# Gates spread by transposes of a broadcast column, the third group's y tiles rounded in one go, and one more drain of GpSimd

## The chip, the core and the metric

The kernel runs on one core of one Trainium2 chip. The metric is the device time of one execution in microseconds (us). Engines: PE is TensorE, ACT is ScalarE, DVE is VectorE, POOL is GpSimd, SP is SyncE, which here issues the plain DMAs. PEld is TensorE's weight load.

## The reference

Three layers follow each other: chunked attention with memory tokens, a top-1 mixture of experts, and an MLP with a SiLU. The change lies in the third, and in how the second's result reaches it. With N = 3072 tokens, D = 512, and a hidden width of 2048:

```python
def _moe_ref(x, expert_emb, tau, w1, w2):
    ...                                   # logits, argmax, softmax
    gate_w = probs[np.arange(N), expert_idx]
    for e in range(E):
        mask = expert_idx == e
        h = np.maximum(x[mask] @ w1[e], 0.0)
        out[mask] = gate_w[mask, None] * (h @ w2[e])

def _moe2_ref(x, w_in, w_out):
    h = x @ w_in
    g = h * (1.0 / (1.0 + np.exp(-h)))
    return (g @ w_out).astype(np.float32)
```

The gate of a token, gate_w, is one number. Here it is multiplied in ahead of the third layer, onto y = h @ w2[e].

## The kernel before, in words

Precision comes from splitting: a float32 tile is written as a high part rounded to fp32r and a low part, the rest, and each product is three matmuls, high x high, high x low and low x high (`three`, L101 to L103; `split`, L96 and L97).

The mixture of experts leaves y in DRAM (`ys`), transposed, in the order of the experts' slots; `names_d` holds which token stands at each place, and `gd` the gate of each token. The third layer takes the tokens in NG = 6 groups of GT2 = 512 (TG = 4 blocks of 128). Group 0 is gated and turned before; its tiles lie in `yt[0]`. For a group g >= 1 these steps are made:

- `load_names(g)`: SP loads the 512 token names to `tok_i`; `load_y(g)`: SP loads 1 MB of y to `yraw`, as KD = 4 blocks of 128 x 512 (model dimension on partitions, tokens on columns).
- `pick_gates(g)`: GpSimd gathers the gates of the 4 x 128 tokens from `gd` to four columns of `gt` (tokens on partitions), one indirect DMA a column.
- To multiply y, the gates must lie along the columns, the same on all 128 partitions. For g = 1, `diagonal` and `spread_gates` do it: ScalarE scales the identity's rows by the gates, and a matmul with a tile of ones sums the columns into `bank[0]`. For g >= 2, `list_gates` has SP store `gt` to DRAM (`gates_d`) and `load_gates` loads it back to `ygate[g]`, repeated over the partitions.
- `gate_y(g, k)`: VectorE multiplies block k of `yraw` by `ygate[g]` (L1270). `high_y` (ScalarE, L1273) and `low_y` (VectorE, L1277) write the rounded tiles to `yt[g % 2]`.

Groups 0 to 2 run through a loop of NI2 = 48 steps i, one for each group and block f of 128 hidden units; the order is `steps`: group 0 for f = 0 to 7, group 1, group 0 for f = 8 to 15 (i = 24 to 31), group 2 from i = 32. A step is written out by hand: what `prep[i]` holds; `up(i + 1)` (12 matmuls of 512 columns to `bank[2]` or `bank[3]`, then the sigmoid on ScalarE, L1216); `silu(i + 1)` (VectorE, L1221) and `halves(i + 1)` (the split to gh and gl); `add(i, c)` for the four blocks of tokens (12 matmuls to `bank[4]` to `bank[7]`); and what `late[i]` holds. `bank[0]` and `bank[1]` are free in the loop. `yt[0]` holds group 0 until `up(31)` and group 2 from `up(32)` on, so at i = 30 the tiles of group 2 are rounded between the two. In steps 22 to 31 VectorE and ScalarE also build mixed weights (`mix`, `mix_halves`).

Groups 3 to 5 (GM = 3) run through `product(q)`, NP2 = 8 products a group, each for two blocks of hidden units. `up2` makes seven half-size products (`seven`: 6 matmuls of 256 columns each) to the left halves of `bank[0]` to `bank[3]` and the right halves of `bank[0]` to `bank[2]`; the right half of `bank[3]` is free. Their mixed weights come from `mixed_d` through a ring of five slots, three in `ring` and two in `y0` (shown as y): `load_mixed(q)` has SP load 256 KB for each of four slots two products ahead (L1386), each waiting for the matmuls that read the slot before. `after_q[q]` lists what product q does ahead of its `up2`: for the group that comes next (g = 4 and 5) the names and y at product 1, pick_gates and list_gates at 2, load_gates at 3, gate_y at 4 and 5. At a group's end `give` copies each block of 128 tokens out of its bank and GpSimd scatters it to `out` by an indirect DMA (L1244). L1595 is the call of the kernel: what shows there at the end are the drains and the barrier behind the program.

All engines take their instructions in the order of this code. SP issues a DMA only when what it waits for is done, and all that SP has to issue stands behind it.

Of the kernel before, what the change touches and what calls it, by code (L numbers as in the profile page):

```python
# [59 lines left out]
def tile_chunk_attention_top1_moe_silu_mlp(ctx, tc, qT, kT, vW, emb, tau, wm, wo, out):  # L60
# [11 lines left out]
    gates_d = dram.tile([N, 1], F32, name="gates_d")  # L72
# [1117 lines left out]
    with ExitStack() as a:  # L1190
# [12 lines left out]
        ygate = [None, bank[0]]  # L1203
# [79 lines left out]
        def list_gates(g):  # L1283
            t = (g - 1) * TG
            SP.dma_start(
                out=gates_d[t * P:(t + TG) * P].rearrange("(c p) o -> p (c o)", p=P), in_=gt[:, 0:TG]
            )

        def load_gates(g):
            at = (g - 1) * GT2  # L1290
            SP.dma_start(out=ygate[g], in_=gates_d[at:at + GT2].rearrange("n o -> o n").to_broadcast([P, GT2]))

        diag, ones = held[0].rearrange("p (c t) -> p c t", c=TG), held[1][:, 0:P]

        def diagonal():
            for c in range(TG):
                ACT.activation(diag[:, c], ident, AF.Copy, scale=gt[:, c:c + 1])

        def spread_gates():
            for c in range(TG):  # L1300
                PE.matmul(bank[0][:, c * P:(c + 1) * P], ones, diag[:, c], start=True, stop=True)

        POOL.memset(ones, 1.0)
# [6 lines left out]
        prep[4].append(diagonal)  # L1310
        late[4].append(spread_gates)
# [8 lines left out]
        for g in range(2, GM + 1):  # L1320
            at = 8 if g == 2 else (g - 1) * NF2 + 1
            prep[at].append(lambda g=g: load_names(g))
            prep[at].append(lambda g=g: load_y(g))
            for n, do in enumerate((pick_gates, list_gates, load_gates)):
                prep[at + (2, 4, 16 if g == 2 else 7)[n]].append(lambda g=g, do=do: do(g))
            if g == 2:
                plan_parts(g, [(gate_y, k) for k in range(KD)], 26, 1)
            elif g == GM:
                plan_parts(g, [(gate_y, k) for k in range(KD)], at + 8, 2)
# [8 lines left out]
        def sums():  # L1338
            less = lambda to, x, y: DVE.tensor_tensor(to, x, y, op=ALU.subtract)
            t1, t2, t4 = (block(t) for t in (held[3], ygate[GM], r_o[3]))  # L1340
            less(t1, quarter(1), quarter(0))
            less(quarter(1), quarter(3), quarter(1))
            yield
            less(t2, quarter(3), t1)
            less(t4, quarter(2), t2)
            yield

        def cast_block(n):
            src = (quarter(0), block(ygate[GM]), block(held[3]), quarter(1), quarter(2), quarter(3), block(r_o[3]))[n]
# [53 lines left out]
        after_q = defaultdict(list)  # L1403
        for g in range(GM + 1, NG):
            q = (g - GM - 1) * NP2
            for n, do in (1, load_names), (1, load_y), (2, pick_gates), (2, list_gates), (3, load_gates):
                after_q[q + n].append(lambda g=g, do=do: do(g))
            for k in range(KD):
# [55 lines left out]
        def product(q):  # L1464
# [9 lines left out]
            if p < NP2 - 1:  # L1474
# [8 lines left out]
                for n in range(2):  # L1483
                    add2(q, n)
                    halves2(q + 1, n)
                    if last:
                        for b in range(3) if n == 0 else range(3, 7):
                            cast_block(b)
                return
            if g < NG - 1:  # L1490
                add2(q, 0)
                add2(q, 1)
                for c in range(TG):
                    give(g, c)

# [13 lines left out]
        for i in range(NI2):  # L1509
# [6 lines left out]
            if i == 2 * NF2 - 2:  # L1516
                for k in range(2):
                    high_y(2, k)
                    low_y(2, k)
            if i == HF - 1:  # L1520
# [8 lines left out]
            elif i + 1 < NI2:  # L1529
                silu(i + 1)  # L1530
                halves(i + 1)
            if i == coding[-1] + 1:
# [3 lines left out]
                ygate += [op.tile([P, GT2], F32, name="ygate")] * (NG - 2)  # L1536
# [9 lines left out]
            if i == 2 * NF2 - 2:  # L1546
                for k in range(2, KD):
                    high_y(2, k)
                    low_y(2, k)
# [49 lines left out]
```

## Time and profile before

| | |
|---|---|
| median of 3 runs | 995.09 us (992.78 to 995.28) |
| the profiled execution | 994.45 us, of which its span 992.6 us |
| busy TensorE / weight loads | 949.7 us (96%) / 849.2 us |
| busy VectorE / ScalarE / GpSimd | 717.2 / 474.6 / 148.1 us |
| TensorE's granted clock, mean | 0.993 |
| third layer: loop of groups 0 to 2 | from 464 us to about 728 us of the span |
| third layer: products of groups 3 to 5 | from about 728 us to about 983 us |

How to read it: the span runs from the first to the last instruction. Busy times are sums over the span; a matmul's end is modelled, so TensorE's stops are seen best in the starts of its matmuls. A wait names the engine that waited, its line, and what released it. SPq, POOLq and the like are an engine's sequencer: it issues DMAs, waits and drains, and the engine isn't counted as busy.

### The profile page before, as it was taken

The numbers are of one execution on the slowest core, as the hardware profiler recorded it, in microseconds if no ns is written. First come the engines' busy times: TensorE is split into PE (matmuls) and PEld (weight loads), VectorE is DVE, ScalarE is ACT, GpSimd is POOL, SyncE is SP. The second block draws the span as 40 slices with busy tenths as digits, with TensorE's granted clock in tenths as the row PEclk, the third lists the DMA queues.
The fourth block names the chain that finished last, engine by engine and source line by source line (L and its number), as shares of the span: only waits on it lengthen the run. The fifth ranks groups of instructions, "written<-read, shape, count | busy, mean of one in ns | idle before, by whom it ended". The sixth has DMA issues, their size and how long they took to land. (4 is left out here: it accounts for less than half of the span.)

```text
span 992.6 us, 19281 instructions
## 1 busy us (share of the span) xinstructions
PE 949.7 (96%) x7182; PEld 849.2 (86%) x7182; DVE 717.2 (72%) x1477; ACT 474.6 (48%) x925; POOL 148.1 (15%) x215
## 2 busy tenths in 40 slices
PE   6998989999999999998999999999998999999996
PEld 4776778999999999998888888788888989889994
DVE  8887797667777888896979986775464666566561
ACT  8896655445456666665454433332332233233231
POOL 8464122011030000010100001030012002001001
PEclk9999999999999999999999999999999999999998
DMA  8997646557477777874423313245053426634321
GB/s 298 365 364 249 247 157 227 177 193 234 129 252 241 249 261 257 274 255 163 147 86 80 113 54 127 86 170 127 0 179 104 124 79 190 128 92 133 122 76 42
DMA packets 65666, 169.97 MB, mean 171 GB/s; under 512 B 12246, under 2 KB 17936, under 8 KB 64536
## 3 DMA queue, kind: packets, MB, share of 16 engines
q1 hardware_dynamic: 60312, 153.91, 47.2%
q0 software_dynamic: 5248, 14.70, 4.6%
q8 instruction: 60, 0.98, 0.4%
q14 instruction: 46, 0.38, 0.2%
HBM read 141.02 MB, written 27.58 MB: 170 GB/s over the span
## 5 line engine op out<-in xcount | busy, mean ns | idle before, releaser
L101 PE MATMUL bank<-hhl,v2h 128*128 128x256 f32 (+1 forms) x352 | 105.0, 298 | 0.0
L102 PE MATMUL bank<-hll,v2h 128*128 128x256 f32 (+1 forms) x352 | 103.2, 293 | 0.0
L103 PE MATMUL bank<-hhl,v2l 128*128 128x256 f32 (+1 forms) x352 | 103.0, 293 | 0.0
L103 PE MATMUL bank<-w2bh,gl 128*128 128x512 f32 x224 | 87.2, 389 | 0.0
L101 PE MATMUL bank<-w2bh,gh 128*128 128x512 f32 x224 | 87.2, 389 | 0.0
L102 PE MATMUL bank<-w2bl,gh 128*128 128x512 f32 x224 | 87.2, 389 | 0.0
L1429 DVE TENSOR_TENSOR held<-held,bank 128x256 f32<-128x256 f32 x168 | 64.7, 418 | 28.8 <-PE bank L103 27.6
L186 ACT ACTIVATE hhl<-bank 128x256 fp32r<-128x256 f32 (+1 forms) x88 | 36.3, 412 | 91.9 <-PE bank L103 89.1
L97 DVE TENSOR_TENSOR w1l<-raw,w1h 128x512 fp32r<-128x512 f32 x106 | 72.6, 685 | 7.8 <-ACT w1h L96 4.9
L1244 POOL DMA_INDIRECT out_dram<-o,tok_i x20 | 20.4, 1019 | 380.6 <-DVE o L1241 324.0
L1216 ACT ACTIVATE sg<-bank 128x512 f32<-128x512 f32 x48 | 28.7, 598 | 100.5 <-PE bank L103 100.5
L187 DVE SCALAR_TENSOR_TENSOR hll<-bank,hhl 128x256 fp32r<-128x256 f32 (+1 forms) x88 | 40.2, 457 | 49.2 <-ACT hhl L186 48.8
L1420 ACT ACTIVATE sp<-held 128x512 f32<-128x512 f32 x48 | 29.5, 630 | 90.6 <-DVE held L1429 89.4
L97 DVE TENSOR_TENSOR v2l<-raw,v2h 128x512 fp32r<-128x512 f32 x106 | 72.7, 686 | 0.0
L101 PE MATMUL bank<-y,w2bh 128*128 128x512 f32 (+1 forms) x210 | 72.0, 343 | 0.0
L97 DVE TENSOR_TENSOR gl<-sp,gh 128x512 fp32r<-128x512 f32 x44 | 30.4, 692 | 57.5 <-ACT gh L96 57.4
L102 PE MATMUL bank<-y,w2bh 128*128 128x512 f32 (+1 forms) x210 | 71.9, 343 | 0.0
L103 PE MATMUL bank<-y,w2bl 128*128 128x512 f32 (+1 forms) x210 | 71.9, 343 | 0.0
L101 PE MATMUL bank<-xhl,w1h 128*128 128x256 f32 (+1 forms) x224 | 68.0, 304 | 2.5 <-PEq L1181 1.5
L152 POOL DMA_INDIRECT xrowl<-xd,rows_i x28 | 30.9, 1103 | 253.9 <-PE bank L174 211.8
L103 PE MATMUL bank<-xhl,w1l 128*128 128x256 f32 (+1 forms) x224 | 67.8, 303 | 0.2 <-DVE w1l L97 0.2
L102 PE MATMUL bank<-xll,w1h 128*128 128x256 f32 (+1 forms) x224 | 67.6, 302 | 0.0
(363 smaller groups left out, 2890.8 us busy)
## 6 DMA issues: line engine op xcount, KB each, us to landing
raw<-in_wm_dram SPq DMA_DIRECT2D x108, 512.0 KB, 4.1
coded<-in_wo_dram SPq DMA_DIRECT2D x36, 512.0 KB, 5.0
ring<-mixed_d SPq DMA_DIRECT2D x58, 256.0 KB, 3.9
vbuf<-in_vW_dram SPq DMA_DIRECT2D x32, 390.0 KB, 5.5
y<-mixed_d SPq DMA_DIRECT2D x38, 256.0 KB, 3.7
mixed_d<-stage SPq DMA_DIRECT2D x8, 1024.0 KB, 3.9
k<-in_kT_dram SPq DMA_DIRECT2D x16, 400.0 KB, 6.6
q<-in_qT_dram SPq DMA_DIRECT2D x16, 384.0 KB, 5.7
```

The lines of the kernel that those rows point to most:

```text
L97: eng.tensor_tensor(lo, src, hi.bitcast(F32), op=ALU.subtract)
L101: PE.matmul(out, lhsT=lh, rhs=rh, start=start, stop=False)
L102: PE.matmul(out, lhsT=lh, rhs=rl, start=False, stop=False)
L103: PE.matmul(out, lhsT=ll, rhs=rh, start=False, stop=stop)
L152: POOL.indirect_dma_start(out=s.where["row"][:, c], out_offset=None, in_=xd[0:LEAD * P] if s in pre else xd, in_offset=IndirectOffsetOnAxi ...
L186: ACT.activation(hh, h, AF.Relu)
L187: DVE.scalar_tensor_tensor(hl, h, 0.0, hh.bitcast(F32), op0=ALU.max, op1=ALU.subtract)
L1216: ACT.activation(sg, h, AF.Sigmoid)
L1244: POOL.indirect_dma_start(out=out, out_offset=IndirectOffsetOnAxis(ap=(tok_i[:, (g - 1) * TG + c:] if g else pre_i[:, c:])[:, 0:1], axis=0 ...
L1420: ACT.activation(out, src, AF.Sigmoid)
L1429: add = lambda to, x, y: DVE.tensor_tensor(to, x, y, op=ALU.add)
```

## The change

Gates of every group g >= 1 are spread by four transposes: the column `gt[:, c]`, read 128 times as a 128 x 128 tile, is transposed on TensorE with the identity. For g = 1, 2 and 3 they go to `bank[0]`, `bank[1]` and `bank[0]` in `late[4]`, `late[24]` and `late[39]`, and gate_y reads the bank. For g = 4 and 5 `spread_half` makes two transposes into the free half of `bank[3]` and ScalarE copies them to `ygate[g]`; the first pair stands ahead of the `up2` of product 3, the second at that product's end. `diagonal`, the tile of ones, `list_gates`, `load_gates` and `gates_d` go. At i = 30 all four `high_y` stand right behind `up(31)`, then two `low_y`, `silu(31)`, two `low_y`, `halves(31)`; the second half of them stood behind `add(30)`. Behind the gives of g = 4 GpSimd gets a `drain`.

```diff
--- before.py
+++ after.py
@@ -69,7 +69,6 @@
     xd = dram.tile([N, DM], F32, name="xd")
     ys = dram.tile([P, KD, N], F32, name="ys")
     names_d = dram.tile([N, 1], I32, name="names_d")
-    gates_d = dram.tile([N, 1], F32, name="gates_d")
     mixed_d = dram.tile([NF2 // 2, P, 4, DM], F32, name="mixed_d")
     gd = dram.tile([N, 1], F32, name="gd")
     td = dram.tile([(NA + 3 * N3) * P, 1], I32, name="td")
@@ -1200,7 +1199,7 @@
         yraw = wp.tile([P, KD, GT2], F32, name="yraw")
         gs = {}
         held = [hp.tile([P, DM], F32, name=f"held{c}") for c in range(TG)]
-        ygate = [None, bank[0]]
+        ygate = [None, bank[0], bank[1], bank[0]]
         HF = NF2 // 2
         steps = [(0, f) for f in range(HF)] + [(1, f) for f in range(NF2)] + [(0, f) for f in range(HF, NF2)]
         steps += [(g, f) for g in range(2, NG) for f in range(NF2)]
@@ -1280,35 +1279,17 @@
             for c in range(TG):
                 pick_gate(c, tok_i[:, (g - 1) * TG:])
 
-        def list_gates(g):
-            t = (g - 1) * TG
-            SP.dma_start(
-                out=gates_d[t * P:(t + TG) * P].rearrange("(c p) o -> p (c o)", p=P), in_=gt[:, 0:TG]
-            )
-
-        def load_gates(g):
-            at = (g - 1) * GT2
-            SP.dma_start(out=ygate[g], in_=gates_d[at:at + GT2].rearrange("n o -> o n").to_broadcast([P, GT2]))
-
-        diag, ones = held[0].rearrange("p (c t) -> p c t", c=TG), held[1][:, 0:P]
-
-        def diagonal():
-            for c in range(TG):
-                ACT.activation(diag[:, c], ident, AF.Copy, scale=gt[:, c:c + 1])
-
-        def spread_gates():
-            for c in range(TG):
-                PE.matmul(bank[0][:, c * P:(c + 1) * P], ones, diag[:, c], start=True, stop=True)
-
-        POOL.memset(ones, 1.0)
+        def spread_gates(to, part=range(TG)):
+            for n, c in enumerate(part):
+                PE.transpose(to[:, n * P:(n + 1) * P], gt[:, c:c + 1].to_broadcast([P, P]), ident)
+
         load_y(1)
         up(0)
         silu(0)
         halves(0)
         prep, late = defaultdict(list), defaultdict(list)
         prep[1].append(lambda: pick_gates(1))
-        prep[4].append(diagonal)
-        late[4].append(spread_gates)
+        late[4].append(lambda: spread_gates(ygate[1]))
         parting = [(gate_y, 0), (high_y, 0), (gate_y, 1), (high_y, 1), (low_y, 0), (gate_y, 2), (high_y, 2), (low_y, 1)]
         parting += [(gate_y, 3), (high_y, 3), (low_y, 2), (low_y, 3)]
 
@@ -1321,8 +1302,8 @@
             at = 8 if g == 2 else (g - 1) * NF2 + 1
             prep[at].append(lambda g=g: load_names(g))
             prep[at].append(lambda g=g: load_y(g))
-            for n, do in enumerate((pick_gates, list_gates, load_gates)):
-                prep[at + (2, 4, 16 if g == 2 else 7)[n]].append(lambda g=g, do=do: do(g))
+            prep[at + 2].append(lambda g=g: pick_gates(g))
+            late[24 if g == 2 else at + 6].append(lambda g=g: spread_gates(ygate[g]))
             if g == 2:
                 plan_parts(g, [(gate_y, k) for k in range(KD)], 26, 1)
             elif g == GM:
@@ -1337,7 +1318,7 @@
 
         def sums():
             less = lambda to, x, y: DVE.tensor_tensor(to, x, y, op=ALU.subtract)
-            t1, t2, t4 = (block(t) for t in (held[3], ygate[GM], r_o[3]))
+            t1, t2, t4 = (block(t) for t in (held[3], wide, r_o[3]))
             less(t1, quarter(1), quarter(0))
             less(quarter(1), quarter(3), quarter(1))
             yield
@@ -1346,7 +1327,7 @@
             yield
 
         def cast_block(n):
-            src = (quarter(0), block(ygate[GM]), block(held[3]), quarter(1), quarter(2), quarter(3), block(r_o[3]))[n]
+            src = (quarter(0), block(wide), block(held[3]), quarter(1), quarter(2), quarter(3), block(r_o[3]))[n]
             to = (Y11, Y2, Y1, Y3, Y21, Y22, Y4)[n]
             ACT.copy(block(to[0]), src)
             DVE.tensor_tensor(block(to[1]), src, block(to[0]).bitcast(F32), op=ALU.subtract)
@@ -1400,11 +1381,19 @@
         for n in range(2):
             prep[NI2 - 6].append(lambda n=n: next(adding[GM]))
 
-        after_q = defaultdict(list)
+        after_q, late_q = defaultdict(list), defaultdict(list)
+
+        def spread_half(g, n):
+            to = bank[3][:, QT:]
+            spread_gates(to, range(2 * n, 2 * n + 2))
+            ACT.copy(ygate[g][:, n * QT:(n + 1) * QT], to)
+
         for g in range(GM + 1, NG):
             q = (g - GM - 1) * NP2
-            for n, do in (1, load_names), (1, load_y), (2, pick_gates), (2, list_gates), (3, load_gates):
+            for n, do in (1, load_names), (1, load_y), (2, pick_gates):
                 after_q[q + n].append(lambda g=g, do=do: do(g))
+            for n, at in enumerate((after_q, late_q)):
+                at[q + 3].append(lambda g=g, n=n: spread_half(g, n))
             for k in range(KD):
                 after_q[q + 4 + k // 3].append(lambda g=g, k=k: gate_y(g, k))
             for n in range(2):
@@ -1486,12 +1475,16 @@
                     if last:
                         for b in range(3) if n == 0 else range(3, 7):
                             cast_block(b)
+                for do in late_q[q]:
+                    do()
                 return
             if g < NG - 1:
                 add2(q, 0)
                 add2(q, 1)
                 for c in range(TG):
                     give(g, c)
+                if g == NG - 2:
+                    POOL.drain()
 
         def hold_halves(q):
             for sg, to in zip(gs[q], (Y11, Y2)):
@@ -1514,9 +1507,14 @@
             if i + 1 < NI2:
                 up(i + 1)
             if i == 2 * NF2 - 2:
+                for k in range(KD):
+                    high_y(2, k)
                 for k in range(2):
-                    high_y(2, k)
                     low_y(2, k)
+                silu(i + 1)
+                for k in range(2, KD):
+                    low_y(2, k)
+                halves(i + 1)
             if i == HF - 1:
                 for c in range(TG):
                     add(i, c)
@@ -1526,14 +1524,15 @@
                 second_signs(j)
                 silu(i + 1)
                 second_split(j, lambda: halves(i + 1))
-            elif i + 1 < NI2:
+            elif i + 1 < NI2 and i != 2 * NF2 - 2:
                 silu(i + 1)
                 halves(i + 1)
             if i == coding[-1] + 1:
                 dx.close()
                 op = a.enter_context(tc.tile_pool(name="op", bufs=1))
                 r_o = [op.tile([P, DM], F32, name=f"o{c}") for c in range(TG)]
-                ygate += [op.tile([P, GT2], F32, name="ygate")] * (NG - 2)
+                wide = op.tile([P, GT2], F32, name="wide")
+                ygate += [wide] * (NG - 1 - GM)
                 ring = op.tile([P, 3, DM], F32R, name="ring")
                 ring = [ring[:, n] for n in range(3)] + [y0[:, n * GT2 + HOME:(n + 1) * GT2 + HOME] for n in (6, 7)]
             if i != HF - 1:
@@ -1543,10 +1542,6 @@
                         give(g, c)
             for do in late[i]:
                 do()
-            if i == 2 * NF2 - 2:
-                for k in range(2, KD):
-                    high_y(2, k)
-                    low_y(2, k)
         for q in range((NG - GM) * NP2):
             product(q)
```

## Rows read from the trace of the kernel before

**Rows 1.** TensorE's waits, 464 to 983 us: waiter, releaser; total us, times, longest.

```profile
PE bank L101 <- DMA ring<-mixed_d: 3.4, 2, 2.6
PE bank L102 <- DVE y L1277: 0.3, 1, 0.3
PE bank L101 <- ACT y L1273: 0.3, 1, 0.3
```

**Rows 2.** Timeline of SP's DMA queue: start us, length us, engine, line, count.

```profile
753.20 0.37 SPq L1285 DMA_DIRECT2D gates_d<-gt  x1
753.66 1.94 SPq L1386 DMA_DIRECT2D ring<-mixed_d  x2
...
763.29 0.32 SPq L1291 DMA_DIRECT2D ygate<-gates_d  x1
```

**Rows 3.** Timeline of TensorE at its two stops; in brackets idle us before, releaser.

```profile
765.36 0.28 PE L103 MATMUL bank<-y,ring 128*128 128x256 f32 x1
768.27 0.36 PE L101 MATMUL bank<-y,ring 128*128 128x256 f32 x1 [2.63 <-DMA ring<-mixed_d]
...
853.81 0.39 PE L101 MATMUL bank<-y,ring 128*128 128x256 f32 x1 [0.80 <-DMA ring<-mixed_d]
```

**Rows 4.** DMA issues: transfer, queue, count, KB each, median us to landing.

```profile
ring<-mixed_d SPq DMA_DIRECT2D x58, 256.0 KB, 3.9
...
gates_d<-gt SPq DMA_DIRECT2D x4, 2.0 KB, 11.7
```

**Rows 5.** Timeline of TensorE in the first `up` of group 2.

```profile
637.58 0.39 PE L102 MATMUL bank<-y,w2ah 128*128 128x512 f32 x1
637.81 0.39 PE L103 MATMUL bank<-y,w2al 128*128 128x512 f32 x1
...
639.61 0.40 PE L103 MATMUL bank<-y,w2al 128*128 128x512 f32 x1
```

**Rows 6.** Timeline of ScalarE at the same place.

```profile
634.71 1.13 ACT L1273 CAST y<-yraw 128x512 fp32r<-128x512 f32 x2
637.28 0.62 ACT L96 CAST gh<-sg 128x512 fp32r<-128x512 f32 x1 [1.44 <-DVE sg L1221]
637.80 1.14 ACT L1273 CAST y<-yraw 128x512 fp32r<-128x512 f32 x2
```

**Rows 7.** Timeline of VectorE at the same place.

```profile
635.35 1.29 DVE L1277 TENSOR_TENSOR y<-yraw,y 128x512 fp32r<-128x512 f32 x2 [1.08 <-ACT y L1273]
```

**Rows 8.** Timeline of TensorE at four transposes, and at the spreading of group 1.

```profile
330.49 0.60 PE L1133 MATMUL bank<-ident,yfirst 128*128 128x128 f32 x4
330.85 0.37 PE L101 MATMUL bank<-xhl,w1h 128*128 128x256 f32 x1
331.06 0.28 PE L102 MATMUL bank<-xll,w1h 128*128 128x256 f32 x1
...
494.14 1.05 PE L1301 MATMUL bank<-held,held 128*128 128x128 f32 x8
494.95 0.48 PE L101 MATMUL bank<-y,w2bh 128*128 128x512 f32 x1
```

**Rows 9.** The gating of y (line 1270): ns min/median/max, first and last start.

```profile
L1270 DVE TENSOR_TENSOR yraw<-yraw,ygate x16: 680/683/687, 609.6 to 873.8; 128x512 f32<-128x512 f32 x16
...
L1270 DVE TENSOR_TENSOR yraw<-yraw,bank x4: 679/679/680, 496.3 to 502.0; 128x512 f32<-128x512 f32 x4
```

**Rows 10.** Timeline of GpSimd, last group: first and last scatter.

```profile
971.95 0.97 POOL L1244 DMA_INDIRECT out_dram<-o,tok_i  x1 [57.83 <-DVE o L1241]
...
984.18 0.97 POOL L1244 DMA_INDIRECT out_dram<-o,tok_i  x1 [3.03 <-ACT o L1241]
```

**Rows 11.** The end (line 1595): count, ns min/median/max, first and last start.

```profile
L1595 POOLq DRAIN x3: 45/113/7818, 983.9 to 992.3; - x3
L1595 SPq DRAIN x3: 7/7/13, 987.5 to 992.0; - x3
```

**Rows 12.** GpSimd's sequencer behind the gathers of the experts (line 1181), same columns.

```profile
L1181 POOLq INC_SWDGE_SEM x2: 492/688/885, 235.5 to 440.6; - x2
```

## The prediction

> **What bounds the kernel now.** I read the waits of TensorE first, over the stretch from 464 to 983 us in which all the edited code runs. The list has three rows and about 4 us in 519 [rows 1], so TensorE's stream sets the time there: an edit counts only by what it takes out of that stream, puts into it, or does after its last matmul. Next I read TensorE's timeline at those waits [rows 3, 5], from start to start, because the ends of matmuls are modelled. Then the DMA queue of SP, where the transfers stand that TensorE waited for [rows 2], and the table of landing times [rows 4]. Last comes the end of the program, on GpSimd and SP [rows 10 to 12].
>
> **The change part by part.** All prices are those of the profiled execution: 994.45 us, of which 992.6 is its span.
>
> *Gates no longer go through DRAM, groups g = 4 and 5.* In the before kernel SP issues the 2 KB store gates_d<-gt at 753.20, and two loads of ring tiles stand behind it [rows 2]. That store takes 11.7 us to land, although a ring load of 256 KB needs 3.9 [rows 4]. TensorE ran into the second of those ring loads at 765.36 and went on at 768.27 [rows 3], some 13 us after that load was issued (the second of the two from 753.66 on). A matmul of 256 columns starts 0.12 us behind the one before (half of the 0.23 that one of 512 takes in [rows 5]), so the stop cost 2.91 - 0.12 = 2.79 us. The stop of the next group is shown as 0.80 us idle where this one has 2.63 [rows 3]; with the same 0.16 between the two ways of counting it cost 0.96. Both stops have the store ahead of them and go with it: **-3.75 us**. What is late next? A ring load is issued when the matmuls that read its slot are over and is wanted about one product (10 us) later; with 3.9 to land it has some 6 us to spare. The load of token names and the 1 MB load of y stay ahead of ring loads one product earlier, where TensorE waits for nothing now [rows 1]. For g = 2 and 3 the same two DMAs go, and they are in no wait of TensorE [rows 1]: nothing.
>
> *Gates by transposes.* Four transposes of 128x128 move the next matmul by 0.36 us (330.49 to 330.85), and that one is followed after 0.21 in place of 0.12 [rows 8]: 0.45 in all, 0.27 for a pair. In group g = 1 they replace four fp32 matmuls, which the chip runs as eight pieces and which take 0.81 us up to the next start [rows 8]: -0.45. Groups 2 and 3 get four each, +0.90; groups 4 and 5 two pairs each, +1.08. Together **+1.53 us**. No row shows a transpose whose stationary operand is one column read 128 times. From below nothing can be cheaper than the plain one, for it is the same pass over 128 columns; from above I take its whole length, 0.27 us (0.60 for four less three starts of 0.11 [rows 8]), that is 20 x 0.27 - 0.90 = 4.5 us. I take 0.11 each: the shape, the type and the operand's place are those of the row, and weight loads run beside matmuls.
>
> The Trainium skill ("TensorE: Matmul & The Clock Gate", Part 4: PE-mode transpose) puts a transpose inside a kernel at about 275 ns. By that price the sum would lose 20 x 0.275 - 0.90 = 4.6 us, an estimate from that page. The row has the same 0.27 as the length of one, but the next starts after 0.11, so the row decides.
>
> Now TensorE's queue waits at the transposes for the gathers of the gates, and the whole stream stands behind. The store at 753.20 waited for the same gathers [rows 2], and the first pair stands just ahead of the product that stopped at 765.36: 11 us of cover; without it each us of lateness is a us of the run. ScalarE gets two copies of 256 columns for each of the groups 4 and 5, shorter than its casts of 512 columns (1.13 us for two [rows 6]); between two products it waits for TensorE anyway. The multiplication by gates is priced alike from a bank and from SBUF, 679 and 683 ns [rows 9]. The four ScalarE operations and the memset that go for g = 1 had nobody waiting for them. All this at nothing.
>
> *The third group's y tiles, i = 30.* From 637.81 to 639.61 three starts took 1.80 us, where 0.23 each is usual (637.58 to 637.81) [rows 5]: 1.12 lost, on a cast of ScalarE and a subtraction of VectorE [rows 1]. The reason stands on ScalarE: it casts k = 0, 1 at 634.71, idles 1.44 us for VectorE, casts gh, and comes to k = 2, 3 at 637.80 [rows 6]. In the new order all four casts follow each other, 0.57 each: done by 637.0. VectorE starts its subtractions at 635.35, two in 1.29 [rows 7]; then silu, k = 2 and k = 3 at about 0.6 each end near 637.3, 637.9 and 638.5. TensorE without a stop wants the second matmul of k = 2, the first that reads the subtraction's result, at 638.3 and that of k = 3 at 638.9: 0.4 us in hand each time. gl comes some 0.5 us later than now and is wanted near 639.9. So **-1.12 us**, with 0.3 that could stay if VectorE slips.
>
> *The drain.* GpSimd's last drain lasts 7.82 us from 983.9 on [rows 11]. Its last scatter, issued at 984.18, is off the engine at 985.15 [rows 10], so 6.6 us are the drain's own; SP is through its waits at 987.5 [rows 11], and the barrier of the end stands behind GpSimd at 991.8. The added drain lies behind the last scatter of g = 4, ahead of a 57.83 us idle time of GpSimd [rows 10]: hidden, and at most 7.8 us long. What it gives back hangs on what the 6.6 us are. If a drain works off the indirect DMAs since the one before, 44 lie behind it in this stage now (20 gathers of gates, 24 scatters) and 4 then: 6.6 x 4 / 44 = 0.6 us, over at 985.8, before SP. The end then hangs on SP at 987.6: -4.2, and no more. If it is a fixed price behind any indirect DMA, 0. For the first speak the two later drains of the same row, 45 and 113 ns with no indirect DMA in between, and the two INC_SWDGE_SEM of GpSimd, which take longer the second time, 492 and then 885 ns, after more such DMAs [rows 11, 12]; that is little. I take **-4.2 us**, with 0 as the other end.
>
> The sum: -3.75 + 1.53 - 1.12 = -3.34 in TensorE's stream, and -4.2 behind it, is -7.5. From 994.45 that is 986.9; the median of the runs shown lies 0.64 above the profiled execution, so 987.6.
>
> **The rivals.**
> 1. *The last drain is as long as before.* Only TensorE's -3.34 stays: 991.8. For it: no row has a second drain behind indirect DMAs, and the 0.6 us is a rule of three. The Trainium skill ("VectorE: DVE Perf Modes", The DRAIN you can't avoid) knows drains at a program's start and end as boilerplate of about 12 ns, the same for every kernel. Here one takes 7.82 us [rows 11], so the page doesn't describe it; by its rule that such a drain doesn't depend on what the kernel does, the added one would give nothing, which is this rival.
> 2. *The transposes take their whole length*, 4.5 instead of 1.53: 990.6 with the drain's gain, 994.8 without. Against it the starts 0.11 apart [rows 8].
> 3. *Slower: the column read 128 times is slow to load*, so that the load and not the pass sets the pace. At four times the row, 0.44 us each, it is 20 x 0.44 - 0.90 = 7.9 us and TensorE's part +3.0; without the drain's gain 998.1. It decides from 0.44 each if the drain gives nothing, from 0.65 if it gives 4.2. Against it: plain weight loads keep up with 0.11.
> 4. *The stops stay*: the ring loads are late for the names and y loads and not for the store. Then -1.12 + 1.53 = +0.4: 991.3 with the drain's gain, 995.5 without. Against it the 11.7 us of the store and its place in both stops [rows 2, 4].
>
> **How the numbers follow.** Forecast 0.50, rival 1 0.27, rival 2 0.08, rival 3 0.06, rival 4 0.09. The likeliest gives the time, 987.6; its own range is 985.3 to 988.8 (0.3 left at the y tiles, up to 1 us for the transposes, and the runs of before reach 2.3 below their median). Rival 1 takes the range up to 992.9, the parts of rivals 2 and 4 with the drain's gain lie inside, and with some room above rival 1 it goes to 994.0; outside stay rival 3, the other halves of 2 and 4 and the tails, less than 2 in 10. A measurement of this kernel can tell 0.3% from no change, 3.0 us. Faster by more: the forecast 0.49, some 0.6 of rival 1 (3.3 us) 0.15, the halves of 2 and 4 with the drain's gain 0.08: 0.72. Slower: rival 3 and a tail, 0.07. Within: 0.21.
>
> **What would show it.** Right, step by step: no wait of TensorE for ring tiles; none at the first `up` of g = 2; transposes starting 0.11 apart without a wait ahead of them; two drains of GpSimd, the early one long, the last over before SP's waits. Wrong: a last drain of 6 us or more, a wait of TensorE at a transpose, or ring loads that still land 10 us after their issue.

## The result, and the profile after

The changed kernel takes 985.89 us in the median of seven runs (983.1 to 989.2), the kernel before 995.09 in seven runs (992.78 to 996.48). The ratio is 0.9903, with a 95% interval of 0.988 to 0.9927, so 9.65 us are gone (7.3 to 11.9). The forecast was 7.5, a time of 987.6. The profiled execution of the changed kernel is 985.89 us long, 984.2 of it the span; against that of before, 8.56 us less in time and 8.42 in span.

TensorE's waits after, of the stretch from 455 to 983 us (columns as in [rows 1]); the one row lies ahead of the edited part, at the jump into the third layer:

```profile
PE bank L100 <- PEq L1180: 3.0, 1, 3.0
```

All three rows of [rows 1] are gone. SP's DMA queue after, in the place of [rows 2]:

```profile
744.53 1.03 SPq L1367 DMA_DIRECT2D y<-mixed_d  x2
745.94 9.29 SPq L1367 DMA_DIRECT2D ring<-mixed_d  x3
755.62 1.03 SPq L1367 DMA_DIRECT2D y<-mixed_d  x2
```

No store of gates stands ahead of a ring load, and TensorE never stops for a ring tile.

TensorE's timeline after: the four transposes of g = 1, where [rows 8] has the eight pieces; the four of g = 3; the first pair of g = 4, with the matmul ahead of it and the first one behind the product's `up`; and, in the first `up` of group 2, the matmuls from the third of k = 1 to the second of k = 2, where [rows 5] has the stop, and the second of k = 3:

```profile
494.47 0.60 PE L1284 MATMUL bank<-ident,gt 128*128 128x128 f32 x4
494.82 0.48 PE L100 MATMUL bank<-y,w2bh 128*128 128x512 f32 x1
...
638.14 0.39 PE L102 MATMUL bank<-y,w2al 128*128 128x512 f32 x1
638.36 0.39 PE L100 MATMUL bank<-y,w2ah 128*128 128x512 f32 x1
638.59 0.39 PE L101 MATMUL bank<-y,w2ah 128*128 128x512 f32 x1
...
639.27 0.39 PE L101 MATMUL bank<-y,w2ah 128*128 128x512 f32 x1
...
685.96 0.60 PE L1284 MATMUL bank<-ident,gt 128*128 128x128 f32 x4
686.32 0.48 PE L100 MATMUL bank<-y,w2bh 128*128 128x512 f32 x1
...
763.47 0.39 PE L102 MATMUL bank<-w2ah,gl 128*128 128x512 f32 x1
763.70 0.38 PE L1284 MATMUL bank<-ident,gt 128*128 128x128 f32 x2
763.83 0.37 PE L100 MATMUL bank<-y,w2bh 128*128 128x256 f32 x1
764.04 0.28 PE L101 MATMUL bank<-y,w2bh 128*128 128x256 f32 x1
...
768.69 0.39 PE L100 MATMUL bank<-w2bh,gh 128*128 128x512 f32 x1
```

Four transposes move the next matmul by 0.35 (494.47 to 494.82), where the eight pieces took 0.81; a pair moves it by some 0.14 (763.70 to 763.83). The starts of the `up` are 0.22 to 0.23 apart without a gap. None of these rows has a bracket, so no transpose waits for a gather. All transposes together, by line (ns min/median/max, first and last start), on TensorE and on its weight loader:

```profile
L1284 PE MATMUL bank<-ident,gt x20: 271/272/273, 494.5 to 858.0; 128*128 128x128 f32 x20
L1284 PEld LDWEIGHTS bank<-ident,gt x20: 134/135/137, 494.2 to 857.9; 128*128 128x128 f32 x20
```

The drains after: the added one (L1487), and the end of the program, where [rows 11] had 7818 ns on GpSimd; then the scatters next to the two long drains:

```profile
L1487 POOLq DRAIN  x1: 7632/7632/7632, 908.5 to 908.5; - x1
L1590 POOLq DRAIN  x3: 51/113/3160, 979.7 to 983.9; - x3
L1590 SPq DRAIN  x3: 7/7/13, 983.3 to 983.6; - x3
...
908.71 1.12 POOL L1243 DMA_INDIRECT out_dram<-o,tok_i  x1 [4.46 <-ACT gh L95]
...
979.93 0.97 POOL L1243 DMA_INDIRECT out_dram<-o,tok_i  x1 [3.02 <-ACT o L1240]
```

A drain stands in GpSimd's queue from the moment its sequencer reaches it, so its length has the last scatter in it: 908.5 + 7.63 = 916.1 is 6.29 after that scatter left the engine (909.83), 979.7 + 3.16 = 982.9 is 1.96 after (980.90). GpSimd is now done before SP (983.3).

Where the 8.42 us of span come from: both traces, cut at the start of the same instructions. sg0, sg31, ... are the sigmoids of the third layer's steps, sp0, sp8, ... those of the last stage (ScalarE's ACTIVATE to sg and to sp), each counted from 0 in the order of their starts. A group has 16 sp: sp0 to sp16 are the products of group 3, in which group 4 is gated. The stop of group 4 and its first pair lie in sp0-sp8, its second pair in the next stretch; those of group 5 in the two stretches after these.

```
us                    before   after   difference  forecast
start of sg0          467.10   467.44    +0.34       0
sg0  - sg31 (g=1,2)   167.11   167.11     0.00       0      (-0.45 and +0.45)
sg31 - sg32 (i=30)      6.59     5.44    -1.15      -1.12
sg32 - sp0  (g=3)      91.70    92.16    +0.46      +0.45
sp0  - sp8  (group 4)  39.38    36.58    -2.80      -2.52   (-2.79 and a pair)
sp8  - sp16            47.23    47.16    -0.07      +0.27   (a pair)
sp16 - sp24 (group 5)  37.56    36.56    -1.00      -0.69   (-0.96 and a pair)
sp24 - last matmul    126.21   126.20    -0.01      +0.27   (a pair)
last matmul - end       9.71     5.54    -4.17      -4.2
```

sg0 starts between 465.7 and 469.7 in the thirteen profiles of this study, behind a part that no edit touches: 4 us that are not the edits'. So the experiments below are read from sg0 on ("sg0 to the last matmul", to its start: 515.79 us before, 511.21 after), and their whole times stand beside that.

### The profile page after: what moved, and what is told of

It is laid out like the page before. It is cut to its first block, busy times and chain, and to the rows that moved or that the text cites. A ratio compares the mean times of both kernels' runs of the same rounds, so it can differ in the third digit from the quotient of the medians.

```text
span 984.2 us, 19290 instructions
## 1 busy us (share of the span) xinstructions
PE 949.0 (96%) x7194; PEld 848.6 (86%) x7194; DVE 717.4 (73%) x1477; ACT 474.2 (48%) x925; POOL 147.8 (15%) x214
```

## The experiments

**The drain alone, and all but the drain.** The first is the kernel before with the drain, the second the changed kernel without it.

```diff
+                if g == NG - 2:
+                    POOL.drain()
```

> The kernel before with the added drain of GpSimd alone. The sum: the last drain of GpSimd, 7.82 us before, ends before SP's last waits, the end moves by -4.2 us, and nothing else changes: some 990.9 against a median of 995.09. A fixed price behind any indirect DMA: the last drain stays near 7.8 us and the time stays at 995. The stops of TensorE for ring tiles (2.6 and 0.8 us idle) and the one at the third group's y tiles stay in both cases.

> The changed kernel without the added drain. The sum: TensorE's part stays, the last drain is back at 7.8 us and the end 4.2 us later than in the changed kernel: some 990.1. If the drain gave nothing and TensorE's part were larger than read: 986.

Measured: the drain alone 993.11 against 996.45, ratio 0.9957 [0.9937, 0.9978], or 4.3 us (2.2 to 6.3). All but the drain: 990.47, ratio 0.9921 [0.9889, 0.9953]. GpSimd's last drains, in the first and in the second kernel, and the wait that stays in the first:

```profile
L1597 POOLq DRAIN  x3: 51/113/3158, 988.1 to 992.3; - x3
...
L1588 POOLq DRAIN  x3: 45/112/7818, 981.1 to 989.5; - x3
```

```profile
PE bank L101 <- DMA ring<-mixed_d: 3.9, 2, 3.0
```

From the last matmul to the end it is 5.54 or 5.55 in the eight profiles of kernels with the drain and 9.71 or 9.72 in the five without, whatever else is changed. The drain is worth its 4.2 us by itself, and the first rival is out.

**The order of the y tiles alone** (kernel before, step i = 30 in the new order).

```diff
             if i == 2 * NF2 - 2:
+                for k in range(KD):
+                    high_y(2, k)
                 for k in range(2):
-                    high_y(2, k)
                     low_y(2, k)
+                silu(i + 1)
+                for k in range(2, KD):
+                    low_y(2, k)
+                halves(i + 1)
...
-            if i == 2 * NF2 - 2:
-                for k in range(2, KD):
-                    high_y(2, k)
-                    low_y(2, k)
```

> The kernel before with the new order of casts and subtractions at i = 30 alone. The sum: the waits of TensorE for a cast and a subtraction near 638 us go, 1.1 us less from the sigmoid of step 31 to that of step 32 (6.59 us before, 5.44 after), time 994.0; nothing else moves. Rival: VectorE becomes late instead and 0.3 us or more stay.

Measured: 996.47, ratio 1.0001 [0.9976, 1.0027]; an effect of 1.1 us can't be told by times here. The trace tells it: sg31 to sg32 5.44 for 6.59, and the same place of TensorE as [rows 5] without the stop:

```profile
637.62 0.39 PE L103 MATMUL bank<-y,w2al 128*128 128x512 f32 x1
...
638.53 0.39 PE L101 MATMUL bank<-y,w2ah 128*128 128x512 f32 x1
638.76 0.39 PE L102 MATMUL bank<-y,w2ah 128*128 128x512 f32 x1
```

The stops for ring tiles stay in this kernel, and here the profile shows a price of a stop that [rows 3] don't have. Group 4, TensorE, and then time by stretch (columns: stretch, its length, busy PE, PEld, DVE, ACT and POOL with counts, TensorE's granted clock, the busy share of the DMA engines, GB/s):

```profile
764.66 0.28 PE L103 MATMUL bank<-y,ring 128*128 128x256 f32 x1
767.12 0.55 PE L101 MATMUL bank<-y,ring 128*128 128x256 f32 x1 [2.18 <-DMA ring<-mixed_d]
767.47 0.41 PE L102 MATMUL bank<-y,ring 128*128 128x256 f32 x1
767.69 0.41 PE L103 MATMUL bank<-y,ring 128*128 128x256 f32 x1
```

```profile
768.00:769.00 1.00, 1.00 (x7) 1.00 (x7) 0.22 (x1) 0.00 (x0) 0.00 (x0) 0.50 1.04 338
...
771.00:772.00 1.00, 1.00 (x11) 1.00 (x10) 0.74 (x2) 0.00 (x0) 0.00 (x0) 1.00 0.52 182
```

The stop is 2.46 us from start to start, shorter than the 2.91 before, but TensorE comes out of it at a granted clock of 0.50, its lower level of 1.2 GHz. Up to 770.45 its matmuls of 256 columns start 0.21 apart in place of 0.12, some 15 of them: about 1.4 us more. The stretch sp0-sp8 is 40.37, 3.9 us more than it is without a stop. The kernel with the drain alone has a stop of 3.33 up to 770.89, goes on at a clock of 1.00, and has 0.50 from 772.3 to 775.7; its stretch takes 41.01. In the profile of before the clock stays at 1.00 behind its stop.

**Gates of groups 4 and 5 by transposes, and nothing else** (kernel before).

```diff
-            for n, do in (1, load_names), (1, load_y), (2, pick_gates), (2, list_gates), (3, load_gates):
+            for n, do in (1, load_names), (1, load_y), (2, pick_gates):
                 after_q[q + n].append(lambda g=g, do=do: do(g))
+            for n, at in enumerate((after_q, late_q)):
+                at[q + 3].append(lambda g=g, n=n: spread_half(g, n))
...
```

> The kernel before with transposes in place of the DRAM round trip for g = 4 and 5 alone. The sum with the pair's price as forecast (0.27 us each): both stops for ring tiles go, -3.75 + 1.08 = -2.7 us. With the price read from the changed kernel (about 0.05 to 0.1 each): -3.5 us, 991.6. Rival (the stops come from the loads of names and y): the stops stay and the time is 995 or more.

Measured: 992.55, ratio 0.9949 [0.9927, 0.9971], or 5.1 us (2.9 to 7.3). TensorE's waits, all there are behind the start of the third layer:

```profile
PE bank L102 <- DVE y L1277: 0.3, 1, 0.3
PE bank L101 <- ACT y L1273: 0.3, 1, 0.3
```

Both stops are gone, and only those: the fourth rival is out. From sg0 to the last matmul it is 512.27 for 515.79, -3.52. With pairs at 0.27 each it had to be -2.7. That the runs give more than the profiles here fits a stop that lowers the clock in some executions, as above, but the interval holds the 3.5 as well. The ratios of the three parts done alone multiply to 0.9957 x 1.0001 x 0.9949 = 0.9907; the whole change has 0.9903. The fourth part, the transposes of g = 1 to 3, was not run alone; the stretches put it at 0.00 and +0.46.

**Is it the store, or the load behind it?** The store put back into the changed kernel:

```diff
...
-            for n, do in (1, load_names), (1, load_y), (2, pick_gates):
+            for n, do in (1, load_names), (1, load_y), (2, pick_gates), (2, list_gates):
...
+        def list_gates(g):
+            t = (g - 1) * TG
+            SP.dma_start(out=gates_d[t * P:(t + TG) * P].rearrange("(c p) o -> p (c o)", p=P), in_=gt[:, 0:TG])
```

> The changed kernel with the store of the gates to DRAM put back for g = 4 and 5, at its old place and in its old form (512 numbers of 4 bytes, each at its own place); nobody reads what it stores. If the store itself holds up the ring loads behind it: it lands after some 12 us, and TensorE's stops for ring tiles are back, 2.6 and 0.8 us idle, some +3.8 us. If the stops came from SP waiting for the store's landing ahead of the load back: no stops, the time of the changed kernel, 986.

The same bytes to the same tile of DRAM, but each partition's four values side by side, so 128 rows of 16 bytes and not 512 pieces of 4:

```diff
-            SP.dma_start(out=gates_d[t * P:(t + TG) * P].rearrange("(c p) o -> p (c o)", p=P), in_=gt[:, 0:TG])
+            SP.dma_start(out=gates_d[t * P:(t + TG) * P].rearrange("(p c) o -> p (c o)", p=P), in_=gt[:, 0:TG])
```

> As the run before, with the same 2 KB stored as 128 rows of 16 bytes in place of 512 numbers of 4. If the number of pieces sets how long the store holds up the queue: it lands after 4 to 6 us and TensorE has no stop, 986. If any store of less than a row of 512 bytes is as slow: as the run before.

The kernel before with the load but no store: groups 4 and 5 load back what is in DRAM from group 3, and are multiplied by those gates.

```diff
-            for n, do in (1, load_names), (1, load_y), (2, pick_gates), (2, list_gates), (3, load_gates):
+            for n, do in (1, load_names), (1, load_y), (2, pick_gates), (3, load_gates):
...
-            at = (g - 1) * GT2
+            at = (min(g, GM) - 1) * GT2
```

> The kernel before without the store of the gates for g = 4 and 5; the load back stays at its place and fetches the gates of group 3, stored long before, so groups 4 and 5 are multiplied by gates that are not theirs. If the store of 4-byte pieces makes both stops: no waits of TensorE for ring tiles, -3.7 us. If SP's wait for the load back's data, or the load itself, has a part: a stop of 0.5 us or more stays.

The store (as above) and a load of 128 gates behind it, in the changed kernel:

```diff
-            for n, do in (1, load_names), (1, load_y), (2, pick_gates):
+            for n, do in (1, load_names), (1, load_y), (2, pick_gates), (2, list_gates), (3, load_gates):
...
+        def load_gates(g):
+            at = (g - 1) * GT2
+            SP.dma_start(out=d.rearrange("p t e -> p (t e)")[:, 0:P], in_=gates_d[at:at + P].rearrange("n o -> o n").to_broadcast([P, P]))
```

> The changed kernel with the store of the gates and a load back (128 of the 512 gates, into a tile that nobody reads) for g = 4 and 5 at their old places, so that SP again waits for the store to land ahead of the ring loads. Store alone at work: stops of TensorE as in the run with the store alone (one of 1.5 us there, so 0 to 4 us here). SP's wait at work as well: both stops back, 3.5 us or more in sum.

Measured: 990.02 with the store, 984.18 with the store in rows, 990.11 with the load alone (before, beside it, 994.91), 988.8 with both. The stretches of group 4 and of group 5, in us:

```
                        sp0-8   sp16-24   sg0 to last matmul
before                  39.38    37.56        515.79
load alone, no store    36.48    36.51        511.84
after                   36.58    36.56        511.21
after + store           36.56    38.46        513.11
after + store in rows   36.58    36.57        511.27
after + store + load    36.57    38.65        513.42
```

The load alone costs TensorE nothing: without the store the kernel before loses both stops. The store alone brings one of the two back, in group 5, and the same bytes in rows bring none. So the stop is the store's, by its shape. Each of these kernels was profiled once, but all thirteen profiles agree: the five with stores in 4-byte pieces for g = 4 and 5 stop for a ring tile in group 5 (1.08 to 1.55 us from start to start), and the eight without have no such stop. Here is what it does, time by stretch again (the last column is GB/s). Group 4 before, group 4 after, group 5 with the store, group 5 with the store in rows:

```profile
757.00:765.00 8.00, 8.00 (x48) 7.07 (x47) 4.06 (x9) 2.51 (x4) 0.00 (x0) 1.00 0.15 8
```

```profile
757.00:765.00 8.00, 8.00 (x49) 7.01 (x48) 4.06 (x8) 2.92 (x6) 0.00 (x0) 1.00 0.31 111
```

```profile
838.00:848.00 10.00, 10.00 (x66) 9.14 (x65) 6.00 (x12) 2.94 (x6) 0.00 (x0) 1.00 0.20 6
```

```profile
834.00:844.00 10.00, 10.00 (x66) 9.13 (x65) 5.44 (x12) 2.88 (x5) 0.00 (x0) 1.00 0.50 134
```

Ahead of the stops before, 8 GB/s move where ring loads of 256 KB each are under way; without the store it is 111. With the store in rows the same queue moves 134. The trace's DMA packets tell the same one by one. Before, the 512 packets of 4 bytes start within one us (754 to 755). Most reads of 2 KB right behind them are as quick as usual, but from 758 to 765 only 30 start, with a median of 0.46 us and up to 1.59, where 0.084 is usual; in group 5 single ones take up to 4.44. With the store put back there are 30 from 838 to 848, with a median of 1.05. With 128 packets of 16 bytes the median stays at 0.084 behind both stores, and the slowest reads take 0.63 and 1.12; without a store single ones reach 1.1 to 1.8 in these stages as well. The DMA engines are mostly idle in the two slow stretches shown (busy 0.15 and 0.20), so more than the length of these reads holds the loads up, and what it is the trace doesn't show. With the store put back into the changed kernel, TensorE's stop reads:

```profile
PE bank L101 <- DMA y<-mixed_d: 1.2, 2, 1.0
...
851.78 0.36 PE L101 MATMUL bank<-y,y 128*128 128x256 f32 x1 [1.03 <-DMA y<-mixed_d]
```

The stretch grows by 38.46 - 36.56 = 1.9. What stays open is why group 4 escapes in the two changed kernels that have the store again. The slow transfers are there (76 GB/s between 757 and 765 with the store, where the kernel before has 8), but shorter; before, with the drain alone and with the y tiles alone, group 4 stops for 2.91, 3.33 and 2.46 us. The load behind the store adds at most 38.65 - 38.46 = 0.19.

**What a drain's length hangs on.** The changed kernel with one more drain ahead of the third layer, and with its drain one group earlier:

```diff
+        POOL.drain()
         load_y(1)
         up(0)
```

```diff
-                if g == NG - 2:
+                if g == NG - 3:
                     POOL.drain()
```

> The changed kernel with one drain more, at the start of the third layer, where GpSimd idles and 36 indirect DMAs have gone before. Theory 1 (a drain waits for the last landing and then works off all indirect DMAs since the drain before, about 0.06 us each, counted from the program's start): the new drain takes about 2.2 us, and the one behind group 4 falls from 7.63 to about 5.4 us. Theory 2 (counted from the jump before the third layer, 0.11 us each): the new one takes about 0.1 us and the other stays at 7.6. Theory 3 (the first drain behind any indirect DMA is dear, whatever their number): the new one takes 4 us or more and the other only waits for its landing, about 3.2 us. The time is that of the changed kernel, 986, in all three.

> The changed kernel with its drain behind group 3 in place of group 4, so that 12 indirect DMAs and not 4 lie behind it. Theory 1: the last drain ends 12 x 0.06 = 0.7 us behind the last landing, length about 3.7 us in place of 3.16, the end 0 to 0.2 us later. Theory 2: 12 x 0.11 = 1.3 us behind it, length about 4.3, the end 0.8 us later. Theory 3: as in the changed kernel, 3.16.

Measured: 986.39 and 984.74, single times. The drains, of the kernel with two early ones and then of the one with the earlier drain:

```profile
L1286 POOLq DRAIN  x1: 3013/3013/3013, 442.4 to 442.4; - x1
L1488 POOLq DRAIN  x1: 4627/4627/4627, 909.6 to 909.6; - x1
L1591 POOLq DRAIN  x3: 51/113/3163, 980.2 to 984.4; - x3
```

```profile
L1487 POOLq DRAIN  x1: 6507/6507/6507, 825.3 to 825.3; - x1
L1590 POOLq DRAIN  x3: 51/113/3485, 978.6 to 982.8; - x3
```

With the indirect DMAs of GpSimd counted since the drain before, or since the start of the program, and the time counted from the end of the last of them on the engine (or from the drain's start, where that is later):

```
indirect DMAs since the last drain   80    76    68    40    36    12    4
us of drain behind the last one     6.62  6.29  5.64  3.44  3.01  2.27  1.96
```

From 36 on it is 0.083 to 0.086 us for each (6.62 / 80, 5.64 / 68, 3.44 / 40, 3.01 / 36), from the start of the program on. The last packet of the 36 ends at 440.86, 1.6 us ahead of the drain, which still took 3.01, so it isn't a wait for data. Nor is it the time gone by since the drain before, which grows along with the count: behind 76 it is 6.29 in six kernels, whether the last of them leaves the engine at 908.45 or at 918.49. With few, the landing of the last scatter comes late (1.75 us after it leaves the engine in both), and the drain ends 0.21 us behind that with 4 and 0.53 with 12; a rule for so few isn't shown. The theory that counts from the start of the program was right in kind and wrong in size: it expected 2.2 and 5.4 for the two early drains, and 3.01 and 4.63 came, since with 36 and 40 behind them they are nearly alike. The drain behind group 3 leaves 12 for the last one, which costs 3.49 - 3.16 = 0.33 in the drain and nothing in the run, because SP's waits end later (5.54 from the last matmul to the end, as in the changed kernel; SP's first drain starts 0.1 us behind the end of GpSimd's).

**What a pair of transposes costs.** Each pair of groups 4 and 5 done twice, so 28 transposes and not 20:

```diff
             spread_gates(to, range(2 * n, 2 * n + 2))
+            spread_gates(to, range(2 * n, 2 * n + 2))
             ACT.copy(ygate[g][:, n * QT:(n + 1) * QT], to)
```

> The changed kernel with each pair of transposes for g = 4 and 5 made twice. If a transpose takes its start distance of 0.11 us: 8 more make the way from the first sigmoid of the third layer to the last matmul 0.9 us longer (511.2 us in the changed kernel). If the matmuls behind a pair take up most of it, as one pair seemed to show (0.14 us to the next matmul, 0.09 of it back by the end of its product): less than 0.5 us.

Measured: 988.87. The transposes are as long as before,

```profile
L1284 PE MATMUL bank<-ident,gt x28: 271/272/273, 495.7 to 860.7; 128*128 128x128 f32 x28
```

and from sg0 to the last matmul it is 512.93 for 511.21: 1.72 for eight more, 0.21 each, where 0.11 (the distance of their starts) and under 0.06 were the two expectations. Neither holds, and the product itself shows why. From the last matmul of 512 columns ahead of the place to the first one behind the product's `up`, in the kernel with the load alone (no transposes there) and with four:

```profile
763.49 0.39 PE L103 MATMUL bank<-w2ah,gl 128*128 128x512 f32 x1
...
768.66 0.39 PE L101 MATMUL bank<-w2bh,gh 128*128 128x512 f32 x1
```

```profile
764.74 0.39 PE L102 MATMUL bank<-w2ah,gl 128*128 128x512 f32 x1
...
770.35 0.40 PE L100 MATMUL bank<-w2bh,gh 128*128 128x512 f32 x1
```

That is 5.17 without transposes, 5.22 with a pair (763.47 to 768.69 in the changed kernel) and 5.61 with four, so a pair costs 0.05 and four cost 0.44 (four times 5.61 - 5.22 is 1.56 of the 1.72; the rest lies outside these products). Up to the next matmul a pair takes 0.14 and four take 0.35, since starts in a row are 0.11 apart and the matmul behind the last one starts 0.03 after it. The next start comes some 0.09 late behind either. The difference is in the 256-column matmuls of the `up`: they start 0.118 apart without transposes and behind four, but 0.113 apart behind a pair, and some 40 of them give back 0.18. All four pairs of the changed kernel show this, and so do those of the kernel with the gates of groups 4 and 5 alone. Why the matmuls run closer behind a pair stays open.

## Why the prediction was right, point by point

**The bound.** Read rightly. Each edit that was priced by TensorE's stream came out there, or behind its last matmul, and what was put at nothing (the added copies on ScalarE, the gathers that the transposes wait for) shows in no wait. The copy of a half is short and nobody waits behind it; first half of group 4, ScalarE:

```profile
763.67 0.62 ACT L95 CAST gh<-sp 128x512 fp32r<-128x512 f32 x1 [2.10 <-PE bank L101]
764.20 0.37 ACT L1389 COPY wide<-bank 128x256 f32<-128x256 f32 x1
```

**The stops, -3.75.** Right, with the price: before minus the kernel with the load alone is 2.90 + 1.05 us in the two groups' stretches, 3.95. What was not thought of is the clock: in two other profiles with the stops TensorE fell to its lower level at the end of one or 1.4 us behind it, and lost some 1.4 us more. Taking the stops from start to start, and not by the idle time (2.63 and 0.80 in [rows 3]), was worth 0.3 of the 3.75. What the prediction had only inferred from the order of SP's queue and 11.7 us of landing, the four runs with and without the store show. The store doesn't just stand ahead of the ring loads; it slows their reads after it is issued.

**The transposes, +1.53.** Right for four in a row: 0.35 in g = 1 in place of 0.81, and +0.46 in g = 3 for the 0.45 worked out. A column read 128 times as the stationary operand loads in 135 ns and runs 272 ns, with the next start 0.11 later, as for the plain ones; rivals 2 and 3 are out. By the Trainium skill ("TensorE: Matmul & The Clock Gate", Part 4: PE-mode transpose) a bf16 transpose inside a kernel takes about 275 ns; that is its length here too, in float32, but no price in a stream, where four move the next matmul by 0.35. The mis-sized term is the pairs: 1.08 for four of them, where four times 0.05 is 0.2. The prediction took half of the 0.36 of four, and the 0.09 of the late next start, without a row that shows two. The pair moves the next matmul by 0.14 and not by 0.18, and the 0.18 that the matmuls behind it give back was in no row. TensorE's part came to -4.58 and not -3.34; of that 1.24 this term is 0.9, and 0.2 are stops that cost more than the rows gave.

**The y tiles, -1.12.** Right, -1.15. ScalarE's four casts now follow each other, VectorE has two subtractions, silu, and two more (after, ScalarE and then VectorE; answers to [rows 6, 7]):

```profile
635.04 2.17 ACT L1272 CAST y<-yraw 128x512 fp32r<-128x512 f32 x4
...
635.68 1.29 DVE L1276 TENSOR_TENSOR y<-yraw,y 128x512 fp32r<-128x512 f32 x2 [1.08 <-ACT y L1272]
636.89 0.68 DVE L1220 TENSOR_TENSOR sg<-bank,sg 128x512 f32<-128x512 f32 x1
637.49 1.28 DVE L1276 TENSOR_TENSOR y<-yraw,y 128x512 fp32r<-128x512 f32 x2
```

The last subtraction ends at 638.77 and its reader, the second matmul of k = 3, starts at 639.27: 0.5 us in hand, where the prediction had 0.4, and no stop.

**The drain, -4.2.** Right in mechanism and in sum. The step that was off is the count: 44 indirect DMAs at 0.15 us were taken, "in this stage"; it is all 80 since the start of the program at 0.083, as the run with two early drains shows. Both lead to a last drain that ends before SP, and SP sets the end as the prediction said, so the error had no price. The prediction also left out the landing of the last scatter: it has the last drain over 0.6 us after that scatter leaves the engine, and it was 1.96, still 0.4 ahead of SP. Had the added drain stood in a place without cover, 76 indirect DMAs and not 40 would have been the work in it: its 7.63 us are hidden only because GpSimd idles behind it ([rows 10]). The Trainium skill ("VectorE: DVE Perf Modes", The DRAIN you can't avoid) has drains at the end of a program as about 12 ns on all engines, the same for every kernel; SP's three, of 7 to 13 ns, agree with that, but GpSimd's longest is 7.82 us here and 3.16 with another drain ahead of it, so the measurement decides against it for that engine.

**The time.** 985.89 against 987.6: the profiled execution is 1.0 below the 986.9 of the sum, 0.9 of it the 1.24 of TensorE less 0.34 at the start of sg0; the other 0.7, from profiled execution to median, lies within the spread of the runs.

## What to carry to other kernels

Price a stop of TensorE from start to start, and ask of each small DMA what it does to the others: a store of 2 KB in pieces of 4 bytes slowed the loads behind it for 10 us, and the same bytes with each partition's values side by side did not. Where a program ends on GpSimd's drain, a drain put into an idle time of GpSimd takes the work off the end (4.2 us here). Four numbers per partition are spread over all partitions by transposes of a broadcast column for 0.35 to 0.46 us of TensorE's stream, without DRAM.

## What the runs showed of the hardware

- GpSimd's drain takes about 0.083 us for each indirect DMA since the drain before (6.62 us for 80, 3.01 for 36), even if all have landed; with 4 and 12 it takes 1.96 and 2.27 us, of which 1.75 are the landing of the last.
- A store to DRAM in 512 pieces of 4 bytes was followed by some 10 us in which few reads of 2 KB by the DMAs behind it started, and single ones took up to 4.4 us (0.084 is usual); 8 and 6 GB/s were left of more than 110. As 128 pieces of 16 bytes it does next to nothing (134 GB/s).
- TensorE left a stop of 2.46 us at a granted clock of 0.50 (1.2 GHz) in one profile, and fell to 0.50 some 1.4 us behind a stop of 3.33 in another; one of 2.91 us, in the kernel before, was followed by a clock of 1.00.
- Transposes of 128 x 128 in a row start 0.11 us apart, and the matmul behind the last starts 0.03 after it. Behind a pair the matmuls of 256 columns start 0.113 us apart, behind four or none 0.118; 0.113 stands also behind the stop with the y tiles alone, once the clock is back. No run explains it.
